# Attention and two MLP layers on one core: the next block's x is loaded at positions 1 and 6, and the weight jobs follow a table

## The chip, the core and the metric

The kernel runs on one core of one Trainium2 chip. The metric is the device time of the whole program in microseconds (us), the median of three runs. TensorE (PE, with its weight loads as PEld) does the matrix products, VectorE (DVE) and ScalarE (ACT) the elementwise work and the copies out of PSUM, SyncE (SP) issues every DMA. Each engine works through its own list of instructions strictly in order: an instruction that waits holds all that stands behind it.

## The reference

`x` is [8, 8, 512, 64] and `state` [8, 8, 32, 64]; the weights are [512, 2048] and [2048, 512], once for each of two MLP layers.

```
xread = softmax(x @ state^T / 8) @ state
sread = softmax(state @ x^T / 8) @ x
x     = concat([xread, sread]) as 4608 tokens x 512
x     = (s * relu(x @ w_in)^2 + b) @ w_out        # first layer
out   = relu(x @ w_in2)^2 @ w_out2                # second layer
```

## The kernel before

**Precision.** Every float32 product is made of reduced-precision pieces: a value is split into a high part (ACT copies it into the narrower type, "hi") and a low part (DVE subtracts that from the value, "lo"), and a product is three matmuls: hi by hi, hi by lo, lo by hi. So each operand that goes into a product costs one ACT and one DVE instruction first, and TensorE waits for both.

**First layer.** It runs in 144 steps; step i handles one token block j (512 tokens) and one slice f of 128 hidden columns (`order`, line 994). From step 32 on, 16 steps make a block. A step is, in this order: six matmuls `mm1` (L509) into a PSUM tile h; on ACT relu, square and the hi copy of it (`relu2`, L516 to L518); twelve matmuls `mm2` (L539) of the slice of step i-2; and then the side work of that step. The PSUM tiles of h, of the attention's transposes and of the S products share four banks in rotation, so a product can start only when the tile four places before it has been read out.

The side work is entered by `at_step(i, fn, rank)` (L998) and runs in the order of rank within its step. It holds the attention of the next block (`att_exp`, `att_norm`, `att_an`, `att_tp`: two DVE transposes and their split stand at places 11 and 12 of a block, the transposes on TensorE at 13), the product S of state and weights (`s_mm`, L306, split at L115 and L116), the lo part of the step's own slice (`low`, L522, rank 5.5), 32 additions that sum up the columns of w_out (`add_up`, L272) and 16 weight jobs.

A weight job (`sums_job`, L196) prepares one piece of the second layer's weights, which arrive as 64-bit floats: load two raw tiles; for each a magnitude on ACT (L131) and four DVE operations that clamp, shift and set bits (L140 to L151, together a `cut`); four DVE sums of 256 columns (`add`, L240); four hi copies on ACT (L249), four lo subtractions on DVE (L253) and eight stores to DRAM. Before the change, job n starts at step 30 + 6n and all of its operations keep the same distances; cuts, add and hi copies stand at ranks 8 to 8.7, behind the step's other work.

**Second layer.** It works on 34 tiles of 128 tokens in six blocks of 6 tiles (the last has 4) with a seven-product scheme in place of eight (`PRODUCTS`). For each block 8 units of seven products each run first (`product`, L751); then follow 24 positions that only add up results (`share`, L775), which I call the share stage: six matmuls of 384 columns each position, twelve in the first three. The stage's position k uses the kept value e = k (t0 to t4 hold them, five a tile); its hi copy (`g_hi`) stands at position k - 3 and its lo at k - 2. At position k the weights for a place 12 further on are loaded into a ring of 12 slots as soon as the slot is read.

During the share stage the x of the next block is prepared (`ahead`, L935): `x_take` (L692) loads it in two parts of two DMAs each into t0 and t1, whose kept values have been read by then; for the second block the bias is added (`x_bias`, L699, on ACT); `x_sum` makes three sums and a difference on DVE, and `xm_hi` and `xm_lo` split the seven operands on ACT and DVE. All of these are entered at fixed positions after k0, the stage's first, behind the pieces of that position. At position 8 ACT also copies a finished result (`p4`), at 16 another.

Of the kernel before, what the change touches and what calls it, by code (L numbers as in the profile page):

```python
# [27 lines left out]
F32 = mybir.dt.float32  # L28
# [12 lines left out]
P = 128  # L41
# [18 lines left out]
TILES = [(j, t) for j in range(B) for t in range(S // P)]  # L60
TILES[2 * TPB : 2 * TPB] = [(B, t) for t in range(NSR // P)]
PARTS = [TILES[i : i + TPB] for i in range(0, len(TILES), TPB)]

LEAST = 2.0 ** (0x70 - 127) * 65536
MOST = (2 - 2.0**-3 - 2.0**-23) * 2.0 ** (0x8F - 127) * 65536
# [3 lines left out]
def attn_mlp2(ctx: ExitStack, tc: tile.TileContext, xT, xn, st, w_in1, w_out1, w_in2, w_out2, s_in, b_in, out):  # L69
# [63 lines left out]
    def to_f32(*pairs):  # L133

        for dst, raw in pairs:
            nc.vector.tensor_scalar(out=dst, in0=dst, scalar1=LEAST, scalar2=MOST, op0=ALU.max, op1=ALU.min)  # L140
        for dst, raw in pairs:
            d = dst.bitcast(U32)
            nc.vector.tensor_scalar(out=d, in0=d, scalar1=3, scalar2=None, op0=ALU.logical_shift_left)
        for dst, raw in pairs:
            d = dst.bitcast(U32)
            nc.vector.scalar_tensor_tensor(  # L146
                out=d, in0=raw[..., 1], scalar=0x80000000, in1=d, op0=ALU.bitwise_and, op1=ALU.bitwise_or
            )
        for dst, raw in pairs:
            d = dst.bitcast(U32)  # L150
            nc.vector.scalar_tensor_tensor(  # L151
                out=d, in0=raw[..., 0], scalar=29, in1=d, op0=ALU.logical_shift_right, op1=ALU.bitwise_or
            )

    def load_piece(key, src, q, k):
        if key[0] == "o":
# [36 lines left out]
        st.update(key=key, mag=mag, pair=lambda: (st["v"], raw), hi=hi, lo=lo)  # L193
        return st

    def sums_job(key, u):  # L196

        c = {}

        def load():  # L200
            c["raw"] = []
            for d in range(2):
                raw = rawp.tile([P, 512, 2], U32, tag="raw", name=f"{key}r{u}{d}")
                if key == "i2":
                    to = raw.rearrange("p (f i c) t -> p f i (c t)", f=2, i=2)
                    for i in range(2):
                        k = 2 * d + i
                        src = w_in2.bitcast(U32)[k * P : (k + 1) * P, 4 * u * P : 4 * (u + 1) * P]
                        nc.sync.dma_start(out=to[:, :, i], in_=src.rearrange("p (f c) -> p f c", f=2))
                else:  # L210
                    f = 2 * u + d
                    nc.sync.dma_start(
                        out=raw.rearrange("p c t -> p (c t)"), in_=w_out2.bitcast(U32)[f * P : (f + 1) * P]
                    )
                c["raw"].append(raw)
            c["v"] = []

        def cut(d):
            v = vp.tile([P, 512], F32, tag="v", name="v")
            c["v"].append(v)  # L220
            magnitude(v, c["raw"][d])
            to_f32((v, c["raw"][d]))

        def four(t):
            return t.rearrange("p (e c) -> p e c", e=2)

        def add():
            v0, v1 = (four(v) for v in c["v"])
            s = vp.tile([P, 512], F32, tag="v", name="v")
            c["v"].append(s)  # L230
            s = four(s)
            c["h"] = [rawp.tile([P, 4, 2 * P], F32R, tag="raw", name=f"{key}h{u}{e}") for e in range(2)]
            s4 = c["h"][1][:, 3].bitcast(F32)
# [7 lines left out]
            h0, h1 = c["h"]  # L241
            c["parts"] = (
                (v0, h0[:, 0:2], slice(0, 5, 4)), (v1, h0[:, 2:4], slice(2, 7, 4)),
                (s, h1[:, 0:2], slice(1, 4, 2)), (h1[:, 3:4].bitcast(F32), h1[:, 2:3], slice(5, 6)),
            )

        def hi(e):
            v, h, _ = c["parts"][e]
            nc.scalar.activation(out=h, in_=v, func=ACTF.Copy)  # L249

        def lo(e):
            v, h, _ = c["parts"][e]
            nc.vector.tensor_tensor(out=v.bitcast(F32R), in0=v, in1=h.bitcast(F32), op=ALU.subtract)  # L253

        def store(e):
            v, h, where = c["parts"][e]
            to = wi_dr[u][:, where] if key == "i2" else wo_dr[:, where, u]
            nc.sync.dma_start(out=to[:, :, 0], in_=h.bitcast(F32))
            nc.sync.dma_start(out=to[:, :, 1], in_=v)

        return load, cut, add, hi, lo, store

    wsum = sraw[:, :, 4 * NS :]

# [519 lines left out]
    def second_layer(rest):  # L784
# [97 lines left out]
        def results(n):  # L882

            th = half(n)
            k0 = first_of[n, NU]
            end = n + 1 == len(PARTS)
            c = {}

            def copies(name, p):
                def fn():  # L890
                    for t in range(2):
                        c[name, t] = c_tile(op, "o", th)
                        act(c[name, t], acc[p, t][:, :th], ACTF.Copy)
# [24 lines left out]
            job(k0 + 16, copies("u2", 1))  # L918
            for t in range(2):
                job(k0 + 20 + t, lambda t=t: add("u2", 3)(c["u2", t], t))  # L920
            nxt = k0 + 24
            for t in range(2):
                go, put = final("u2", t, 1, 0, add("u2", 2))
                job(nxt, go)
                job(nxt + 1, put)
            if end:
                job(nxt + 3, copies("p5", 2))
                return c, final
            job(nxt + 6, copies("u3", 1))
            for t in range(2):  # L930
                go, put = final("p4", t, 0, 1, lambda v, t: sub(v, c["u3", t], v))
                job(nxt + 9, go)
                job(nxt + 10, put)
                go, put = final("u3", t, 1, 1, add("u3", 2))
                job(nxt + 10, go)  # L935
                job(nxt + 11, put)

        def ahead(n):

            k0 = first_of[n - 1, NU]  # L940
            for d in range(2):
                job(k0 + 4 + 4 * d, lambda d=d: x_take(n, d))
                if n == 1:
                    job(k0 + 7 + 4 * d, lambda d=d: x_bias(d))
            for e, k in enumerate((14, 16, 25, 26)):
                job(k0 + k, lambda e=e: x_sum(n, e))
            for m, hi, lo in ((0, 8, 9), (2, 12, 13), (5, 13, 15), (1, 17, 18), (3, 20, 22), (4, 26, 27), (6, 27, 28)):
                job(k0 + hi, lambda m=m: xm_hi(n, m))
                job(k0 + lo, lambda m=m: xm_lo(n, m))

# [101 lines left out]
    jobs1 = [(key, u) for key in ("i2", "o2") for u in range(NU)]  # L1052
    for n, (key, u) in enumerate(jobs1):
        load, cut, add, hi, lo, store = sums_job(key, u)
        t = place[1, CUTS[1]] + 10 + 6 * n
        at_step(t, load, 7)
# [209 lines left out]
```

## Time and profile before

| what | us |
|---|---|
| median of 3 runs (1386.71 to 1393.24) | 1391.29 |
| profiled execution, its own time | 1387.76 |
| its span, first to last instruction | 1385.9 |
| TensorE busy in the span | 1342.6 |
| DVE busy | 943.1 |
| ACT busy | 824.1 |

The profile describes one execution. A line of the waits names who waited for whom, the total, the number of times and the longest. In a timeline, brackets give the engine's idle time before the instruction and what ended it. Line numbers are those of the kernel before. A line of the windows is start:end and length, then the busy time (instructions) of PE, PEld, DVE, ACT and POOL, then PEclk, the DMA engines' busy share and GB/s. "PEclk" is the clock granted to TensorE as a share of full speed.

### The profile page before, as it was taken

Reading aid. Unit: us, or ns where it says so; the run is one execution under the profiler, and the core shown is the slowest. Engines: PE = TensorE matmul, PEld = TensorE weight load, DVE = VectorE, ACT = ScalarE, POOL = GpSimd, SP = SyncE. Lnnn points to the kernel's source line nnn. Section 1 sums busy time; section 2 is a strip of 40 time slices with the busy share of each in tenths; the row PEclk is TensorE's granted clock in tenths of the full one; section 3 lists DMA queues with packets and bytes.
Section 4 is the critical chain, followed back from the end, with each engine's and each line's share of the span. In section 5 each row is a group of like instructions: output and inputs, shape, how many; then the busy total and the mean of one; then the engine's idle time right before and its main releaser. Section 6 shows DMA issues by size and latency. Waiting matters only on the chain.

```text
span 1385.9 us, 23117 instructions
## 1 busy us (share of the span) xinstructions
PE 1342.6 (97%) x8214; PEld 1186.5 (86%) x8214; DVE 943.1 (68%) x1847; ACT 824.1 (59%) x1620; POOL 0.7 (0%) x7
## 2 busy tenths in 40 slices
PE   6899999999999999999999999999999999999998
PEld 4677777777767777788999899989999998999998
DVE  7888667877575767655656586667568666766765
ACT  4777556666666665766655655545555554555555
POOL 0000000000000000000000000000000000000000
PEclk7999999999999999999999999999999999999999
DMA  7365224362526253334586786687668668766987
GB/s 243 115 225 190 92 70 148 107 202 84 203 98 217 92 175 118 116 136 129 191 283 178 222 247 194 168 257 242 178 208 260 200 172 250 242 180 205 302 268 236
DMA packets 159602, 257.91 MB, mean 186 GB/s; under 512 B 14592, under 2 KB 69888, under 8 KB 158720
## 3 DMA queue, kind: packets, MB, share of 16 engines
q1 hardware_dynamic: 159488, 256.44, 58.8%
q8 instruction: 66, 1.08, 0.3%
q14 instruction: 48, 0.39, 0.1%
HBM read 207.09 MB, written 49.28 MB: 185 GB/s over the span
## 4 chain that ended last, share of the span: by engine, by line
PE 82%; DVE 9%; DMA 4%; ACT 3%; issue 1%; SPq 0%; DVEq 0%; POOLq 0%; POOL 0%; ACTq 0%
PE m L751 24%; PE acc L539 22%; PE p L775 21%; PE h L509 12%; DMA bigt<-x 3%; PE S L306 1%; DVE g L522 1%; DMA wi<-v 1%; PE on L1159 1%; DVE S L116 1%; PE sr L461 1%; DVE s L420 1%; DVE v L146 1%; PE sc L306 0%; DVE t L424 0%
## 5 line engine op out<-in xcount | busy, mean ns | idle before, releaser
L539 PE MATMUL acc<-g,o1h 128*128 128x512 f32 (+1 forms) x1152 | 344.8, 381 | 5.6 <-DVE g L522 5.1
L539 PEld LDWEIGHTS acc<-g,o1h 128*128 128x128 f32 x1152 | 212.6, 189 | 50.1 <-DVE g L522 6.6
L539 PE MATMUL acc<-g,o1l 128*128 128x512 f32 (+1 forms) x576 | 218.4, 379 | 0.6 <-DVE o1l L191 0.6
L509 PE MATMUL h<-aT,S 128*128 128x512 f32 x768 | 204.0, 401 | 5.3 <-DVE aT L435 2.9
L751 PE MATMUL m<-bigx,bigx 128*128 128x384 f32 (+1 forms) x1050 | 199.1, 327 | 0.0
L509 PEld LDWEIGHTS h<-aT,S 128*128 128x128 f32 x768 | 142.5, 191 | 60.7 <-issue 9.1
L751 PEld LDWEIGHTS m<-bigx,bigx 128*128 128x128 f32 x1050 | 177.5, 188 | 0.2 <-DVE bigx L593 0.2
L522 DVE TENSOR_TENSOR g<-r,g 128x512 fp32r<-128x512 f32 (+1 forms) x144 | 94.7, 658 | 76.0 <-ACT g L518 75.7
L590 ACT ACTIVATE sc<-sc 128x384 f32<-128x384 f32 (+1 forms) x144 | 72.8, 505 | 102.1 <-DVE sc L593 100.6
L516 ACT ACTIVATE r<-h 128x512 f32<-128x512 f32 (+1 forms) x144 | 81.9, 569 | 82.0 <-PE h L509 78.5
L539 PEld LDWEIGHTS acc<-g,o1l 128*128 128x128 f32 x576 | 108.9, 189 | 21.4 <-DVE o1l L191 1.1
L751 PE MATMUL m<-bigx,bigring 128*128 128x384 f32 (+1 forms) x660 | 124.9, 326 | 0.0
L775 PE MATMUL p<-g,bigw 128*128 128x384 f32 (+1 forms) x522 | 111.9, 326 | 0.0
L751 PEld LDWEIGHTS m<-bigx,bigring 128*128 128x128 f32 x660 | 111.0, 188 | 0.2 <-DVE bigx L593 0.2
L590 ACT ACTIVATE v<-m 128x384 f32<-128x384 f32 (+1 forms) x96 | 45.5, 474 | 91.9 <-PE m L751 91.2
L593 DVE TENSOR_TENSOR v<-m,r 128x384 f32<-128x384 f32 (+1 forms) x48 | 25.7, 535 | 103.8 <-PE m L751 103.8
L517 ACT ACTIVATE r<-r 128x512 f32<-128x512 f32 (+1 forms) x144 | 87.7, 609 | 4.6
L518 ACT ACTIVATE g<-r 128x512 fp32r<-128x512 f32 (+1 forms) x144 | 87.6, 609 | 4.6
L775 PEld LDWEIGHTS p<-g,bigw 128*128 128x128 f32 x522 | 89.7, 189 | 0.0
L116 DVE TENSOR_TENSOR S<-S,S 128x512 fp32r<-128x512 f32 x54 | 34.8, 686 | 69.5 <-ACT S L115 69.5
L775 PE MATMUL p<-g,bigx 128*128 128x384 f32 (+1 forms) x396 | 77.1, 335 | 3.9 <-ACT g L590 2.7
L775 PE MATMUL p<-bigg,bigw 128*128 128x384 f32 (+1 forms) x342 | 73.8, 326 | 0.0
(164 smaller groups left out, 2095.5 us busy)
## 6 DMA issues: line engine op xcount, KB each, us to landing
bigx<-wi SPq DMA_DIRECT2D x200, 256.0 KB, 3.1
bigring<-wi SPq DMA_DIRECT2D x110, 256.0 KB, 3.1
bigx<-wo SPq DMA_DIRECT2D x108, 256.0 KB, 3.1
bigring<-wo SPq DMA_DIRECT2D x66, 256.0 KB, 3.1
i1r<-w_in SPq DMA_DIRECT2D x16, 512.0 KB, 5.2
xn<-xn SPq DMA_DIRECT2D x8, 1024.0 KB, 8.7
o1r<-w_out SPq DMA_DIRECT2D x16, 512.0 KB, 4.3
x<-ot SPq DMA_DIRECT2D x32, 256.0 KB, 3.0
```

The source lines that it names most:

```text
L116: nc.vector.tensor_tensor(out=lo, in0=src, in1=hi.bitcast(F32), op=ALU.subtract)
L146: nc.vector.scalar_tensor_tensor(out=d, in0=raw[..., 1], scalar=0x80000000, in1=d, op0=ALU.bitwise_and, op1=ALU.bitwise_or)
L509: nc.tensor.matmul(out=hp, lhsT=l_, rhs=r_, start=(i == 0), stop=(i == len(ops) - 1))
L516: nc.scalar.activation(out=r, in_=hp, func=ACTF.Relu)
L517: nc.scalar.activation(out=r, in_=r, func=ACTF.Square)
L518: nc.scalar.activation(out=g[:, 0], in_=r, func=ACTF.Copy)
L522: nc.vector.tensor_tensor(out=g[:, 1], in0=r, in1=g[:, 0].bitcast(F32), op=ALU.subtract)
L539: nc.tensor.matmul(out=o, lhsT=l_, rhs=r_, start=(opens and i == 0), stop=(closes and i == 2))
L590: nc.scalar.activation(out=c, in_=src, func=func)
L593: nc.vector.tensor_tensor(out=out, in0=x, in1=y, op=op)
L751: nc.tensor.matmul(out=o, lhsT=w[:, a, k, :], rhs=x[:, b, k, :], start=(start and k + a + b == 0), stop=(k + a == 2), skip_group_check=True,)
L775: nc.tensor.matmul(out=o, lhsT=w[:, a], rhs=g[:, b], start=(opens and e == 0), stop=(u == NU - 1 and e == 2), skip_group_check=True,)
```

## The change

The work on each operand and TensorE's own list stay what they are. Moved are: the two x loads of the share stage from positions 4 and 8 to 1 and 6; the bias from 7 and 11 to 9 and 15; the x sums from 14, 16, 25, 26 to 12, 18, 22, 25; the splits of the seven operands; one addition of results by a position. In the first layer `to_f32` is cut in two (`clamp`, `bits`), and every operation of every weight job has its own step from a table of 16 rows of 15 numbers; the loads stand three steps ahead of the magnitude, the stores one step behind each lo. Hi part 1 may stand before `add`. The third tile of a job, and in every second job also the second, is taken from the pool "o" of four buffers, which also serves the block results, instead of "v" with three. The 32 column additions get steps of a table too.

```
+SUMS_AT = (
+    (27, 27, 27, 27, 28, 28, 34, 35, 30, 35, 35, 36, 35, 36, 36),
+    (31, 31, 31, 34, 34, 35, 39, 40, 38, 41, 41, 42, 40, 42, 43),
...
+        def temp(e):
+            pool, tag = (op, "o") if e == 2 or (e == 1 and n % 2) else (vp, "v")
+            v[e] = pool.tile([P, 512], F32, tag=tag, name="v")
...
+        steps = []
+        for d in range(2):
+            pair = lambda d=d: (v[d], c["raw", d])
+            steps += [lambda d=d: mag(d), lambda p=pair: clamp(p()), lambda p=pair: bits(p())]
+        steps += [add]
+        steps += [lambda e=e: hi(e) for e in range(4)]
+        steps += [lambda e=e: lo(e) for e in range(4)]
+        return load, steps, store
...
-                job(k0 + 4 + 4 * d, lambda d=d: x_take(n, d))
+                job(k0 + (1, 6)[d], lambda d=d: x_take(n, d))
                 if n == 1:
-                    job(k0 + 7 + 4 * d, lambda d=d: x_bias(d))
-            for e, k in enumerate((14, 16, 25, 26)):
+                    job(k0 + (9, 15)[d], lambda d=d: x_bias(d))
+            for e, k in enumerate((12, 18, 22, 25)):
                 job(k0 + k, lambda e=e: x_sum(n, e))
-            for m, hi, lo in ((0, 8, 9), (2, 12, 13), (5, 13, 15), (1, 17, 18), (3, 20, 22), (4, 26, 27), (6, 27, 28)):
+            for m, hi, lo in ((0, 9, 10), (3, 12, 13), (2, 16, 17), (1, 19, 20), (4, 25, 26), (5, 26, 27), (6, 27, 28)):
...
-    for k in range(32):
-        at_step(place[1, CUTS[1]] + 1 + 9 * k // 8, lambda k=k: add_up(k), 6)
+    for k, n in enumerate(ADDS_AT):
+        at_step(n, lambda k=k: add_up(k), 6)
...
+    for n, when in enumerate(SUMS_AT):
+        load, steps, store = sums_job(n)
         for d in range(2):
-            at_step(t + 2 + d, lambda cut=cut, d=d: cut(d), 8)
-        at_step(t + 4, add, 8)
+            at_step(when[3 * d] - 3, lambda load=load, d=d: load(d), 7)
+        for e, (t, fn) in enumerate(zip(when, steps)):
+            at_step(t, fn, 8 + (e == 6) / 2 + (7 <= e < 11) / 4)
         for e in range(4):
-            at_step(t + 4 + e // 2, lambda hi=hi, e=e: hi(e), 8.5)
-            at_step(t + 5 + e // 2, lambda lo=lo, e=e: lo(e), 8.7)
-            at_step(t + 6 + e // 2, lambda store=store, e=e: store(e), 9)
+            at_step(when[11 + e] + 1, lambda store=store, e=e: store(e), 9)
```

**SP in the first share stage.** The DMA list before: `bigring`, `bigg` and `bigx` are ring slots loaded from the weights (`wo`), `bigt0` and `bigt1` take the next block's x.

```order
L648 DMA bigring_6397<-wo_120 128x512 x4
L648 DMA bigg_6653<-wo_120 128x512
L648 DMA bigx0_6105<-wo_120 128x512
L697 DMA bigt0_6554<-x1_1_122 128x2x256
L697 DMA bigt0_6554<-x1_2_123 128x2x512
L648 DMA bigx1_6106<-wo_120 128x512
L648 DMA bigx2_6107<-wo_120 128x512
L902 DMA out_0<-o_7545 128x384
L648 DMA bigx3_6238<-wo_120 128x512
L902 DMA out_0<-o_7547 128x384
L648 DMA bigx4_6239<-wo_120 128x512
L697 DMA bigt1_6555<-x1_1_122 128x2x256
```

The same place of SP's list now:

```order
L682 DMA bigring_6397<-wo_120 128x512 x3
L731 DMA bigt0_6554<-x1_1_122 128x2x256
L731 DMA bigt0_6554<-x1_2_123 128x2x512
L682 DMA bigring_6397<-wo_120 128x512
L682 DMA bigg_6653<-wo_120 128x512
L682 DMA bigx0_6105<-wo_120 128x512
L682 DMA bigx1_6106<-wo_120 128x512
L682 DMA bigx2_6107<-wo_120 128x512
L936 DMA out_0<-o_7545 128x384
L731 DMA bigt1_6555<-x1_1_122 128x2x256
```

The first part of x stands three ring loads earlier, the second part two.

**ACT in the first share stage.** Before: `g0`, `g1`, `g2`, `bigg` are hi copies of kept values, `o` a result, `bigx` an operand of the next block, `bigt0<-bigt0,cs` the bias.

```order
L590 ACTIVATE g2_6772<-bigt2_6618 128x384
L703 ACTIVATE bigt0_6554<-bigt0_6554,cs_109 128x768 x2
L590 ACTIVATE o_7631<-p40_7516 128x384
L590 ACTIVATE o_7633<-p41_7520 128x384
L590 ACTIVATE g0_6659<-bigt2_6618 128x384
L590 ACTIVATE bigx0_6105<-bigt0_6554 128x768
L590 ACTIVATE bigg_6653<-bigt2_6618 128x384 x2
```

Now:

```order
L624 ACTIVATE g2_6772<-bigt2_6618 128x384
L624 ACTIVATE o_7631<-p40_7516 128x384
L624 ACTIVATE o_7633<-p41_7520 128x384
L624 ACTIVATE g0_6659<-bigt2_6618 128x384
L624 ACTIVATE bigg_6653<-bigt2_6618 128x384
L737 ACTIVATE bigt0_6554<-bigt0_6554,cs_109 128x768 x2
L624 ACTIVATE bigx0_6105<-bigt0_6554 128x768
L624 ACTIVATE bigg_6653<-bigt2_6618 128x384
```

The first instruction that needs x has moved behind the result's copies and two more hi copies of kept values.

**DVE at steps 75 and 76 of the first layer.** Before: `v_3845` and `v_3881` are the two raw tiles of weight job 7, `v_3916` its sum, `an` the attention's transposes, `g` the lo part of a slice.

```order
L140 TENSOR_SCALAR v_3881<-v_3881 128x512
L143 TENSOR_SCALAR v_3881<-v_3881 128x512
L146 SCALAR_TENSOR_TENSOR v_3881<-i2r71_3753,v_3881 128x512
L151 SCALAR_TENSOR_TENSOR v_3881<-i2r71_3753,v_3881 128x512
L430 STREAM_TRANSPOSE an_3911<-t1_3741 128x512
L435 TENSOR_TENSOR aT5_3875<-an_3911,aT5_3875 128x512
L522 TENSOR_TENSOR g_3895<-r_3894,g_3895 128x512
L240 TENSOR_TENSOR v_3916<-v_3845,v_3881 128x256
```

Now (the job's tiles are `v_3698`, `v_3735` and the sum `v_3896`):

```order
L165 SCALAR_TENSOR_TENSOR v_3735<-i2r71_3598,v_3735 128x512
L170 SCALAR_TENSOR_TENSOR v_3735<-i2r71_3598,v_3735 128x512
L464 STREAM_TRANSPOSE an_3884<-t1_3688 128x512
L469 TENSOR_TENSOR aT5_3883<-an_3884,aT5_3883 128x512
L556 TENSOR_TENSOR g_3867<-r_3866,g_3867 128x512
L265 TENSOR_TENSOR v_3896<-v_3698,v_3735 128x256
L265 TENSOR_TENSOR v_3896<-v_3896,v_3698 128x256
L265 TENSOR_TENSOR v_3698<-v_3698 128x256
L265 TENSOR_TENSOR i2h71_3894<-v_3735,v_3896 128x256
L464 STREAM_TRANSPOSE an_3925<-t1_3767 128x512
```

The job's add has moved ahead of the second transpose; its second tile is finished before the first one.

## Rows read from the trace of the kernel before

**Rows 1.** The page: busy time, share of the span and instructions of each engine.

```profile
PE 1342.6 (97%) x8214; PEld 1186.5 (86%) x8214; DVE 943.1 (68%) x1847; ACT 824.1 (59%) x1620; POOL 0.7 (0%) x7
```

**Rows 2.** Waits of TensorE: who, for whom, us in total, times, longest.

```profile
PE p L775 <- ACT g L590: 8.5, 4, 3.2
```

**Rows 3.** Windows, first-layer blocks from step 32: length, busy (instructions), clock, DMA.

```profile
191.33:268.53 77.20, 75.11 (x443) 57.82 (x441) 60.06 (x114) 45.10 (x80) 0.00 (x0) 0.98 0.40 131
268.53:344.89 76.36, 74.83 (x451) 57.53 (x449) 54.64 (x103) 50.79 (x91) 0.00 (x0) 1.00 0.43 145
344.89:424.16 79.27, 75.92 (x443) 57.59 (x442) 50.84 (x98) 48.49 (x86) 0.00 (x0) 0.98 0.44 152
424.16:497.95 73.79, 73.49 (x443) 56.66 (x441) 49.93 (x97) 47.74 (x84) 0.00 (x0) 1.00 0.41 138
497.95:573.17 75.22, 73.78 (x443) 56.66 (x441) 49.98 (x94) 49.87 (x89) 0.00 (x0) 1.00 0.43 146
```

**Rows 4.** Windows: ten positions of the first share stage, then five whole stages.

```profile
772.68:786.23 13.55, 13.55 (x79) 13.55 (x79) 9.49 (x20) 7.54 (x17) 0.00 (x0) 1.00 0.61 176
772.68:806.90 34.22, 30.44 (x163) 27.77 (x163) 23.46 (x44) 22.56 (x45) 0.00 (x0) 1.00 0.75 232
895.44:928.93 33.49, 30.90 (x163) 29.45 (x163) 23.37 (x44) 19.48 (x41) 0.00 (x0) 0.95 0.75 236
1017.45:1050.69 33.24, 30.07 (x163) 27.82 (x163) 23.36 (x44) 19.48 (x41) 0.00 (x0) 1.00 0.76 238
1139.21:1173.21 34.00, 31.17 (x163) 29.09 (x163) 23.37 (x44) 19.49 (x41) 0.00 (x0) 0.95 0.77 233
1261.73:1292.54 30.81, 29.32 (x164) 27.82 (x163) 21.79 (x44) 18.41 (x41) 0.00 (x0) 1.00 0.76 239
```

**Rows 5.** Timeline, first share stage: start us, us, engine, instruction [idle before].

```profile
781.64 1.36 SPq L697 DMA_DIRECT2D bigt<-x  x2
...
787.64 1.76 ACT L703 ACTIVATE bigt<-bigt,cs 128x768 f32<-128x768 f32 x2 [5.01 <-DMA bigt<-x]
...
790.04 0.52 ACT L590 ACTIVATE g<-bigt 128x384 fp32r<-128x384 f32 x1
...
790.62 1.57 PE L775 MATMUL p<-g,bigring 128*128 128x384 f32 x6 [3.18 <-ACT g L590]
```

**Rows 6.** Timeline, fourth share stage, ACT and DVE.

```profile
1156.29 0.84 ACT L590 ACTIVATE bigx<-bigt 128x768 fp32r<-128x768 f32 x1 [4.50 <-DMA bigt<-x]
...
1157.16 0.96 DVE L593 TENSOR_TENSOR bigx<-bigt,bigx 128x768 fp32r<-128x768 f32 x1 [4.78 <-ACT bigx L590]
```

**Rows 7.** DMA issues: count, KB each, median us from issue to landing.

```profile
x<-ot SPq DMA_DIRECT2D x32, 256.0 KB, 3.0
...
bigt<-x SPq DMA_DIRECT2D x10, 512.0 KB, 6.2
```

**Rows 8.** Timeline, first layer, steps 75 to 77.

```profile
405.20 0.42 DVE L140 TENSOR_SCALAR v<-v 128x512 f32<-128x512 f32 x1
...
407.46 0.70 DVE L430 STREAM_TRANSPOSE an<-t 128x512 f32<-128x512 f32 x1
...
410.07 1.21 DVE L240 TENSOR_TENSOR v<-v 128x256 f32<-128x256 f32 x3
...
411.32 1.15 ACT L249 ACTIVATE i2h<-v 128x512 fp32r<-128x512 f32 x2 [2.49 <-DVE v L240]
...
413.00 1.34 PE L306 MATMUL S<-V,st 64*32 64x512 f32 x14 [2.40 <-ACT r L516]
```

**Rows 9.** Windows: after two idle stretches of TensorE, and steps 69 and 70.

```profile
787.00:796.00 9.00, 5.56 (x29) 4.48 (x27) 3.24 (x6) 7.43 (x13) 0.00 (x0) 1.00 0.97 347
915.47:918.88 3.41, 3.41 (x13) 3.41 (x12) 0.70 (x2) 1.30 (x3) 0.00 (x0) 0.50 1.01 378
367.72:378.00 10.28, 10.28 (x70) 7.18 (x69) 5.64 (x11) 6.78 (x12) 0.00 (x0) 1.00 0.60 202
```

**Rows 10.** Timeline, first layer, step 69, ACT.

```profile
370.59 0.66 ACT L131 ACTIVATE v<-i2r 128x512 f32<-128x512 f32 x1 [3.46 <-DMA wi<-v]
```

More of the change, by code (lines that the diff above doesn't have):

```diff
@@ L62 @@
 PARTS = [TILES[i : i + TPB] for i in range(0, len(TILES), TPB)]
+SUMS_AT = (
[16 rows of a table added]
+)
+ADDS_AT = (
+    24, 26, 26, 29, 29, 29, 30, 30, 30, 30, 30, 31, 31, 32, 32, 32, 32, 32, 33, 34, 35, 35, 36, 36,
+    37, 37, 37, 38, 44, 45, 46, 46,
+)
 LEAST = 2.0 ** (0x70 - 127) * 65536
@@ L143, in to_f32, with bits @@
             nc.vector.tensor_scalar(out=d, in0=d, scalar1=3, scalar2=None, op0=ALU.logical_shift_left)
+    def bits(*pairs):
         for dst, raw in pairs:
@@ L153, in to_f32 @@
             )
+    def to_f32(*pairs):
+        clamp(*pairs)
+        bits(*pairs)
     def load_piece(key, src, q, k):
@@ L194, in piece, with sums_job, load, mag @@
         return st
-    def sums_job(key, u):
+    def sums_job(n):
+        key, u = ("i2", "o2")[n // NU], n % NU
         c = {}
[L200 to L224, printed above, removed]
+        v = c["v"] = [None] * 3
+        def load(d):
+            raw = c["raw", d] = rawp.tile([P, 512, 2], U32, tag="raw", name=f"{key}r{u}{d}")
+            if key == "i2":
+                to = raw.rearrange("p (f i c) t -> p f i (c t)", f=2, i=2)
+                for i in range(2):
+                    k = 2 * d + i
+                    src = w_in2.bitcast(U32)[k * P : (k + 1) * P, 4 * u * P : 4 * (u + 1) * P]
+                    nc.sync.dma_start(out=to[:, :, i], in_=src.rearrange("p (f c) -> p f c", f=2))
+            else:
+                f = 2 * u + d
+                nc.sync.dma_start(
+                    out=raw.rearrange("p c t -> p (c t)"), in_=w_out2.bitcast(U32)[f * P : (f + 1) * P]
+                )
+        def temp(e):
+            pool, tag = (op, "o") if e == 2 or (e == 1 and n % 2) else (vp, "v")
+            v[e] = pool.tile([P, 512], F32, tag=tag, name="v")
+        def mag(d):
+            temp(d)
+            magnitude(v[d], c["raw", d])
+        def two(t):
@@ L225, in four, with his @@
             return t.rearrange("p (e c) -> p e c", e=2)
+        def his():
+            if "h" not in c:
+                c["h"] = [rawp.tile([P, 4, 2 * P], F32R, tag="raw", name=f"{key}h{u}{e}") for e in range(2)]
+            return c["h"]
         def add():
[L228 to L232, printed above, removed]
@@ L233, in add @@
-            s4 = c["h"][1][:, 3].bitcast(F32)
+            temp(2)
+            v0, v1, s = (two(x) for x in v)
+            s4 = his()[1][:, 3].bitcast(F32)
             for out, x, y, fn in (
@@ L240, in add, with part @@
                 nc.vector.tensor_tensor(out=out, in0=x, in1=y, op=fn)
[L241 to L245, printed above, removed]
+        def part(e):
+            h0, h1 = his()
+            if e == 3:
+                return h1[:, 3:4].bitcast(F32), h1[:, 2:3], slice(5, 6)
+            h = (h0[:, 0:2], h0[:, 2:4], h1[:, 0:2])[e]
+            return two(v[e]), h, (slice(0, 5, 4), slice(2, 7, 4), slice(1, 4, 2))[e]
         def hi(e):
-            v, h, _ = c["parts"][e]
-            nc.scalar.activation(out=h, in_=v, func=ACTF.Copy)
+            x, h, _ = part(e)
+            nc.scalar.activation(out=h, in_=x, func=ACTF.Copy)
         def lo(e):
-            v, h, _ = c["parts"][e]
-            nc.vector.tensor_tensor(out=v.bitcast(F32R), in0=v, in1=h.bitcast(F32), op=ALU.subtract)
+            x, h, _ = part(e)
+            nc.vector.tensor_tensor(out=x.bitcast(F32R), in0=x, in1=h.bitcast(F32), op=ALU.subtract)
         def store(e):
-            v, h, where = c["parts"][e]
+            x, h, where = part(e)
             to = wi_dr[u][:, where] if key == "i2" else wo_dr[:, where, u]
             nc.sync.dma_start(out=to[:, :, 0], in_=h.bitcast(F32))
-            nc.sync.dma_start(out=to[:, :, 1], in_=v)
-        return load, cut, add, hi, lo, store
+            nc.sync.dma_start(out=to[:, :, 1], in_=x)
+        steps = []
[6 more added lines that the diff above has]
+        return load, steps, store
     wsum = sraw[:, :, 4 * NS :]
@@ L919, in results @@
             for t in range(2):
-                job(k0 + 20 + t, lambda t=t: add("u2", 3)(c["u2", t], t))
+                job(k0 + 21 + t, lambda t=t: add("u2", 3)(c["u2", t], t))
             nxt = k0 + 24
@@ L1048, in attn_mlp2 @@
             at_step(step(B, 0) + 4 * q + k - 6, lambda q=q, k=k: lo_v1(q, k), 5)
-    for k in range(32):
-        at_step(place[1, CUTS[1]] + 1 + 9 * k // 8, lambda k=k: add_up(k), 6)
+    for k, n in enumerate(ADDS_AT):
+        at_step(n, lambda k=k: add_up(k), 6)
     at_step(step(BIASED, 0) + 14, lambda: colsum(), 2)
[L1052 to L1056, printed above, removed]
+    for n, when in enumerate(SUMS_AT):
+        load, steps, store = sums_job(n)
         for d in range(2):
-            at_step(t + 2 + d, lambda cut=cut, d=d: cut(d), 8)
-        at_step(t + 4, add, 8)
+            at_step(when[3 * d] - 3, lambda load=load, d=d: load(d), 7)
+        for e, (t, fn) in enumerate(zip(when, steps)):
+            at_step(t, fn, 8 + (e == 6) / 2 + (7 <= e < 11) / 4)
         for e in range(4):
-            at_step(t + 4 + e // 2, lambda hi=hi, e=e: hi(e), 8.5)
-            at_step(t + 5 + e // 2, lambda lo=lo, e=e: lo(e), 8.7)
-            at_step(t + 6 + e // 2, lambda store=store, e=e: store(e), 9)
+            at_step(when[11 + e] + 1, lambda store=store, e=e: store(e), 9)
     def cut_sread():
```

2 lines of the change are left out of this document (1 added, 1 removed), and 14 rows, old and new, of the table SUMS_AT.

## The prediction

> **What bounds the kernel now.** I read the page's first part first: TensorE is busy 1342.6 of 1385.9 us [rows 1], and the change leaves its list alone. So the time can only move by what TensorE loses between its instructions. The waits of TensorE come next: the largest sum in them is 8.5 us in four waits of the share stage on ACT's hi copies [rows 2]. Gaps alone do not tell what is lost, since matmuls that are fed just in time count as busy while they stretch. So I took the length of equal stretches of work from the windows, with the ends read off TensorE's timeline.
>
> First layer: four of the five blocks from step 32 show the same 443 matmuls, the fourth needs 73.79 us and 73.49 of them busy [rows 3]. Against 73.49 the five blocks lose 3.71, 2.87, 5.78, 0.30 and 1.73, together 14.39 us.
>
> Share stages: the first ten positions of the first stage, 78 matmuls, take 13.55 us [rows 4], which is 0.1737 each. A stage to its end has 162 (three positions of 12, 21 of 6), so 28.14 us. The five stages take 34.22, 33.49, 33.24, 34.00 and 30.81 [rows 4] and lose 6.08, 5.35, 5.10, 5.86 and 2.67, together 25.06 us.
>
> So 39.45 us are within this change's reach. The work itself stays, so against the profiled execution's own 1387.76 us the floor is 1348.3. The median shown, 1391.29, is 3.5 higher; I add nothing for that, since a kernel with fewer stalls has fewer of them to vary.
>
> Here the Trainium skill bears on how to count: "Perfetto Trace Analysis", in "Identifying the Most-Contended Engine", says that the busy share of matmuls is no good measure of how near TensorE is to its limit and points to the weight loads. The third stage agrees: PE is busy 30.07 of 33.24 us, PEld 27.82, near the 28.14 of my count [rows 4]. By PE's idle time alone only 8.72 us (first layer) and 13.86 us (stages) would be in reach.
>
> **The x loads, step by step.** The first part of x is issued at 781.64 and the bias behind it starts when it has landed, at 787.64; ACT stood idle 5.01 us for it, since 782.63. Behind it stands the hi copy that TensorE needs, which starts at 790.04, and TensorE starts again at 790.62 after 3.18 us of idling [rows 5]. In the fourth stage, without a bias, it is the x copy that waits 4.50 us, since 1151.79 [rows 6]. I take that as the cause in all five stages.
>
> Now the load stands at position 1 instead of 4. Position 4 ends 48 matmuls after k0, at 781.0, and the issue came 0.6 later. Position 1 ends after 24 matmuls, at 4.17; with the same 0.6 the load is issued 4.8 us after k0, in the first stage at 777.4. With the 6.0 from issue to use it is there at 10.8 after k0. As an upper bound I take both issues (1.36 [rows 5]) and the median landing of 6.2 [rows 7] one after the other, 7.6: then it is there at 12.4. Its first user has moved behind the result's copies and two hi copies. In the fourth stage ACT was ready for the x copy at 1151.79 - 1139.21 = 12.58 after the stage's start, with one hi copy (0.52 [rows 5]) less ahead of it, so now at 13.1. The load is 0.7 to 2.3 us early; ACT waits for nothing there.
>
> The second part is issued at the end of position 6 (60 matmuls, 10.42, plus 0.6 is 11.0) and is there by 18.6 at most. Its first user stands at position 15 (18.8) or 16 (19.8). Both fit, the first barely. The ring loads that the x loads now pass on SP are 12 positions ahead of their use, and the first positions last twice as long; I cost this at nothing. If that cover went, a late slot would show as TensorE waiting for a DMA.
>
> What is late next? After the x copy (0.84) and its own 0.52 the next hi copy is done at 14.5, and with DVE's 0.96 for the x lo [rows 6] ahead of it the piece's lo about 15.5. Position 13 needs it at 96 matmuls, 16.7. So stages two to five hold, with 1 us to spare; I leave 0.3 each, 1.2. The first stage also has two biases of 1.76 [rows 5]: hi at 16.2, lo at 17.2, and the third matmul needs it at 17.0. From there ACT and DVE are at the limit, with three more splits and the second bias to come. The bounds are 0 and all of 6.08 left; I take 2.5. So 25.06 - 3.7 = 21.4 us come back.
>
> **The weight jobs.** The longest gap of the third block shows what is wrong. DVE cuts the job's second tile from 405.20, turns the attention's second half from 407.46 and only then, at 410.07, makes the job's add. ACT's hi copies wait for the add until 411.32, and behind them stands the read-out of h, whose PSUM bank TensorE needs: it starts at 413.00 after 2.40 us, that is, it could have started at 410.60 [rows 8]. In the new list the cut (2.26) is already done and the turn with the slice's lo (2.61) stands behind the add. So the add starts 4.87 us earlier, at 405.2, and is done at about 406.7. The turn follows, with ACT's half of it done by 408.1; the two hi copies (1.15) and a short one (0.4) end at 409.7 and the read-out at 410.3, before 410.60. This gap goes, with little to spare.
>
> The other gaps have the same form: DVE gets a cut and an add in the very steps where the attention fills it. On average there is room, since DVE is busy 50 to 60 us of a block [rows 3]. A load that comes late does no harm by itself: ACT waited 3.46 us for one in step 69 [rows 10], and TensorE was busy throughout steps 69 and 70 [rows 9].
>
> New in the table is a wait: the result copies of a block need four "o" buffers, and a job still holds one or two. In four blocks (steps 49, 65, 81, 97) the fourth copy, on ACT, takes the buffer of the first and waits for its store, 3.0 us in the median [rows 7]. Behind it stand the split of S and the next relu. At steps 49 to 52 the load of job 4 stands behind the attention's loads as well. Bounds: 0, since the 3.46 above cost nothing, and 4 x 3.0 = 12. I take the nearer row and leave 1.6. So 14.39 - 1.6 = 12.8 come back.
>
> **Sum.** 1387.76 - 21.4 - 12.8 = 1353.6; I say 1353.5.
>
> The clock is in these numbers already: after its waits in the second stage TensorE ran from 915.47 at 0.50 of full speed, 1.2 in place of 2.4 GHz, for 3.41 us [rows 9], about 1.7 us lost; after the 3.18 us in the first stage it kept 1.00 [rows 5, 9]. The Trainium skill ("TensorE: Matmul & The Clock Gate", Part 1) has the clock fall when the engine has idled; the trace shows that this need not follow. By the rule alone, 2.5 us left in one gap of the first stage would bring 1.7 more, 1355.2.
>
> **Rivals.**
> The table only moves the stalls. For it: in four blocks a new wait of 3.0, and the margin of 0.3 us at the gap worked out. Against it: in that gap 4.87 us of DVE work leave the way. If all 14.39 stay: 1387.76 - 21.4 = 1366.4.
>
> The share stage stays bound by its pieces. DVE is busy 23.4 us of a stage that is to take 28.14 [rows 4], in a chain with ACT. If half of the 25.06 stays: 1387.76 - 12.5 - 12.8 = 1362.5. Against it: the positions before the x load ran at full speed with DVE 9.49 of 13.55 busy [rows 4].
>
> Only idle time comes back, the stretched matmuls stay: 22.58 less the 5.3 kept above gives 1370.5. Against it: the weight loads' busy time.
>
> It turns slower. From its first magnitude to its last store a job now takes eight to ten steps in place of five and holds its buffers; if the next job's magnitude, on ACT, waits for a buffer whose store has not landed, relu is held in every job. By the worst gap seen (2.40, and 1.7 of clock) that is 4.1 us in each of 16 jobs, 65.6, in place of 14.39: 1387.76 - 21.4 + 51.2 = 1417.6. It decides from (21.4 + 14.39) / 16 = 2.2 us a job on. Against it: the covered 3.46.
>
> The x loads don't move in time, because DVE reads a kept value of t0 late: then the stages' loss stays, 1387.76 - 12.8 = 1375.0. If the first layer's stays as well, nothing moves, 1384 to 1391.
>
> **Chances.** Forecast 0.65, its own range 1348 to 1360; stalls only moved 0.12; half of the stages' loss stays 0.11; idle time alone 0.03; x loads late 0.02; no change 0.03; slower 0.04. What a measurement can tell from no change is 0.5%, 7 us. Faster 0.65 + 0.12 + 0.11 + 0.03 + 0.02 = 0.93, the same 0.03, slower 0.04. The range 1346 to 1367 takes in the first three cases, and 2 us below the floor for what varies elsewhere.
>
> **What would show it.** The five share stages should take 28 to 29 us, the first about 30.6, and ACT should no longer wait for the DMA of x in any. The blocks of the first layer should take 73.5 to 75, without TensorE idle before S at step 77. Wrong I am if TensorE shows new waits for ACT at the first steps of a block (the "o" buffer), at step 53 (job 4's load), or for pieces from position 13 on in stages without a bias.

## The result, and the profile after

The changed kernel takes 1352.11 us, the median of four runs (1351.20 to 1353.45), against 1389.28 for the kernel before, whose fourth run moved its median from the 1391.29 of three; the ratio is 0.9731, with a 95% interval of 0.9702 to 0.9759. A second group of runs gave 1352.55 against 1389.28. The profiled execution took 1351.20 us with a span of 1349.4, so its span is 36.5 us shorter.

The page's first part answers to [rows 1]. TensorE's busy time has fallen too, by 17.0 us, with the same number of matmuls.

```profile
PE 1325.6 (98%) x8214; PEld 1181.7 (88%) x8214; DVE 942.3 (70%) x1847; ACT 827.8 (61%) x1620; POOL 0.7 (0%) x7
```

The five blocks of the first layer, the changed kernel's windows with the columns of [rows 3]:

```profile
190.37:264.81 74.44, 73.49 (x443) 56.65 (x442) 60.76 (x114) 46.58 (x83) 0.00 (x0) 1.00 0.38 126
264.81:338.96 74.15, 74.15 (x451) 57.60 (x449) 52.83 (x103) 49.18 (x87) 0.00 (x0) 1.00 0.48 162
338.96:413.48 74.52, 73.64 (x443) 56.74 (x441) 50.14 (x97) 48.51 (x86) 0.00 (x0) 1.00 0.44 147
413.48:486.68 73.20, 73.20 (x443) 56.71 (x441) 49.71 (x96) 50.35 (x88) 0.00 (x0) 1.00 0.44 148
486.68:559.88 73.20, 73.20 (x443) 56.72 (x441) 49.68 (x97) 49.51 (x87) 0.00 (x0) 1.00 0.46 155
```

They take 369.51 us together, 12.33 less than before. And the five share stages, which answer to [rows 4]:

```profile
759.43:789.42 29.99, 29.44 (x164) 27.88 (x163) 22.64 (x42) 22.06 (x44) 0.00 (x0) 1.00 0.82 268
877.82:905.90 28.08, 28.08 (x163) 28.08 (x163) 23.11 (x43) 18.99 (x40) 0.00 (x0) 1.00 0.84 282
994.30:1022.51 28.21, 28.21 (x164) 28.06 (x164) 22.66 (x42) 18.99 (x40) 0.00 (x0) 1.00 0.85 282
1110.92:1139.16 28.24, 28.24 (x163) 28.05 (x163) 22.65 (x42) 18.99 (x40) 0.00 (x0) 1.00 0.85 282
1227.57:1255.66 28.09, 28.09 (x164) 28.09 (x164) 21.93 (x44) 18.37 (x40) 0.00 (x0) 1.00 0.80 264
```

They take 142.61 us, 23.15 less. In the waits of TensorE the largest sum of [rows 2] is gone; what is left of a share stage there is one line:

```profile
PE p L809 <- DVE g L627: 0.5, 2, 0.3
```

Read the first two numbers of a stage's row against each other: in the last four stages PE is busy for the whole length and the length is that of the work, 28.1; no clock below 1.00 is left in either table. 12.33 + 23.15 = 35.48 of the 36.5 us. The other 1.0 lies outside both and is the net of small shifts, among them the start (the first layer's first matmul stands 0.7 us earlier) and the last share stage, which has grown by 0.4.

Why the stages are short is seen in the fourth one, where ACT had waited 4.50 us [rows 6]. The timeline of the changed kernel, SP's queue and ACT:

```profile
1115.69 0.90 SPq L731 DMA_DIRECT2D bigt<-x  x2
...
1123.36 0.52 ACT L624 ACTIVATE g<-bigt 128x384 fp32r<-128x384 f32 x1
1123.78 0.84 ACT L624 ACTIVATE bigx<-bigt 128x768 fp32r<-128x768 f32 x1
```

The load is issued 4.77 us after the stage's start and its first user starts at 12.86, straight behind the copy before it: no idle time in brackets, so nothing was waited for.

At steps 75 to 77 the order of [rows 8] is turned round. The changed kernel's timeline:

```profile
398.67 1.21 DVE L265 TENSOR_TENSOR v<-v 128x256 f32<-128x256 f32 x3
...
400.14 0.70 DVE L464 STREAM_TRANSPOSE an<-t 128x512 f32<-128x512 f32 x1
...
402.45 0.40 ACT L276 ACTIVATE i2h<-i2h 128x256 fp32r<-128x256 f32 x1
402.76 0.57 ACT L550 ACTIVATE r<-h 128x512 f32<-128x512 f32 x1
...
403.95 1.09 PE L340 MATMUL S<-V,st 64*32 64x512 f32 x16
```

The add runs ahead of the transpose, the job's last hi copy ends at 402.85, the read-out of h at 403.33, and S starts at 403.95 without a bracket. Of the 2.40 us nothing is left.

### The profile page after: what moved, and what is told of

It is laid out like the page before. It is cut to its first block, busy times and chain, and to the rows that moved or that the text cites. A ratio compares the mean times of both kernels' runs of the same rounds, so it can differ in the third digit from the quotient of the medians.

```text
span 1349.4 us, 23118 instructions
## 1 busy us (share of the span) xinstructions
PE 1325.6 (98%) x8214; PEld 1181.7 (88%) x8214; DVE 942.3 (70%) x1847; ACT 827.8 (61%) x1620; POOL 0.7 (0%) x7
## 4 chain that ended last, share of the span: by engine, by line
PE 91%; DVE 6%; ACT 2%; issue 1%; DMA 0%; DVEq 0%; POOLq 0%; POOL 0%; ACTq 0%
PE p L809 25%; PE m L785 25%; PE acc L573 25%; PE h L543 13%; PE S L340 2%; PE on L1189 1%; PE sr L495 1%; PE sc L340 0%; PE tp L475 0%; PE S L368 0%; DVE t L443 0%; DVE m L442 0%; DVE S L138 0%; DVE t L438 0%; DVE g L556 0%
## 5 line engine op out<-in xcount | busy, mean ns | idle before, releaser
L556 DVE TENSOR_TENSOR g<-r,g 128x512 fp32r<-128x512 f32 (+1 forms) x144 | 94.6, 657 | 74.1 <-ACT g L552 74.1
L809 PE MATMUL p<-g,bigx 128*128 128x384 f32 (+1 forms) x396 | 73.7, 328 | 0.6 <-DVE g L627 0.5
```

The source lines that it names most:

```text
L556: nc.vector.tensor_tensor(out=g[:, 1], in0=r, in1=g[:, 0].bitcast(F32), op=ALU.subtract)
L809: nc.tensor.matmul(out=o, lhsT=w[:, a], rhs=g[:, b], start=(opens and e == 0), stop=(u == NU - 1 and e == 2), skip_group_check=True,)
```

## The experiments

Medians in us, each beside the kernel before on the same chip (1388.69, 1389.30 and 1389.28 in the three groups); "blocks" and "stages" are the sums of the five windows in the profiled execution. The changed kernel's time is that of the last group, its sums are those shown above.

| kernel | time | ratio, 95% interval | blocks | stages |
|---|---|---|---|---|
| before | 1389.28 | | 381.84 | 165.76 |
| changed | 1352.55 | 0.9732 [0.9715, 0.9748] | 369.51 | 142.61 |
| share stage alone | 1363.60 | 0.9821 [0.9804, 0.9839] | 381.60 | 142.32 |
| table alone | 1378.00 | 0.9918 [0.9902, 0.9935] | 369.26 | 167.32 |
| loads alone | 1372.98 | 0.9882 [0.9861, 0.9903] | 382.41 | 150.48 |
| loads put back | 1362.39 | 0.9807 [0.9791, 0.9823] | 369.69 | 153.91 |
| old adds | 1355.07 | 0.9755 [0.9738, 0.9771] | 371.84 | 142.39 |
| new adds, old jobs | 1365.57 | 0.9821 [0.9805, 0.9838] | 381.74 | 142.60 |

**The two halves apart.** First the share stage on the kernel before:

```diff
-                job(k0 + 4 + 4 * d, lambda d=d: x_take(n, d))
+                job(k0 + (1, 6)[d], lambda d=d: x_take(n, d))
...
-            for e, k in enumerate((14, 16, 25, 26)):
+            for e, k in enumerate((12, 18, 22, 25)):
```

> The kernel before with the share-stage half of the change alone (loads of x at positions 1 and 6, its users moved, the result's second copy one position later); the weight jobs stay as they were. Theory: the two halves work in different stages and add up. The five share stages should be as long as in the changed kernel, 28.1 to 28.3 us and the first 30.0, so 23.1 us less than before, and the first layer's blocks as before, 73.5 to 79.3: 1389.3 - 23.1 = 1366. Rival, the stalls of the first layer also cost the second through the clock or late buffers: the stages keep some of their 25 us and the time is above 1370. Rival, the table carries most of the gain: 1376 or more.

Then the changed kernel with these lines put back:

> The changed kernel with the share stage put back (loads at 4 and 8 and every user where it was); the weight jobs follow the table. Theory: the five blocks of the first layer come out as in the changed kernel (74.4, 74.2, 74.5, 73.2, 73.2), 12.3 us less than before, the share stages as before (34.2, 33.5, 33.2, 34.0, 30.8): 1389.3 - 12.3 = 1377. The sum of the two halves' gains should then be 35.4 of the 37.2 measured. Rival, the stall only moves without the other half: within 3 us of before.

Each half gives back its own stretch: 25.1 and 10.7 us, together 35.8 of 37.2. With the share stage alone the blocks are as before. With the table alone the stages keep all that they lost and take 1.6 us more; 1.1 of that is in the first, where the granted clock is 0.90 in the mean and not 1.00 as before [rows 4]:

```profile
759.35:794.65 35.30, 30.82 (x163) 30.41 (x163) 23.52 (x44) 22.75 (x45) 0.00 (x0) 0.90 0.73 225
```

The first theory holds in both: the halves add up, and no stall of the first layer shows in the second. (What moved by one position in the first of them is DVE's add of the result, not a copy.)

**The load, or the order of its users?** On the kernel before only the first pair of lines above; and on the changed kernel the same pair put back.

> The kernel before with nothing changed but the two loads of x, at positions 1 and 6; the bias, splits and sums stay at their old places. Theory (the load's landing holds ACT): the wait for the first part goes in all five stages. The second part is issued 11.0 us after the stage's start and lands at 17.2 to 18.6, while its first hi copy stands at position 12, whose end is at 16.7: ACT may wait there up to 1.9 us, and the pieces behind it lose about 1 us a stage. So 5 to 10 of the 25.06 us stay, 15 to 20 come back: 1369 to 1374. Rival (the order of the work on ACT and DVE is the cause, the load only shows it): the stages stay at 31 to 34 us, 1385 to 1390. Rival (the load alone is all of it): 28 to 30 us a stage, 1366.

> The changed kernel with the two loads of x back at positions 4 and 8; their users stay where the change put them, as does the table. Theory (the landing decides): the first part is issued 9.0 us after the stage's start and lands at 15.0, ACT is ready for it at 13.1 and waits 1.9 us; position 13 needs its piece at 16.7 and it had about 1 us to spare, so each stage loses about 1 us, the first 3 to 4 in all: 1352.1 + 6 = 1358. Rival (the order alone is enough, since the users moved behind the landing): the stages as in the changed kernel, within 2 us of 1352. Rival (the load's place is everything): the stages back at 31 to 34, 1373 or more.

The stages lose 9.8 us against 5 x 28.14 with the loads alone, and 13.2 with the users alone; before they lost 25.06. So neither is the whole: the loads alone bring 15.3 us, the users alone 11.9, and both 23.15, less than their sum, since they remove parts of one wait. With the loads alone it is the second part that is late: ACT waits 2.9 to 3.7 us for it in each of the five stages, where up to 1.9 was expected, and 0.7 for the first part in the first stage only. Its second stage, SP's queue and ACT:

```profile
904.66 0.96 SPq L697 DMA_DIRECT2D bigt<-x  x2
...
911.96 0.85 ACT L590 ACTIVATE bigx<-bigt 128x768 fp32r<-128x768 f32 x1 [3.66 <-DMA bigt<-x]
```

The landing as the cause is borne out; in the second kernel the size was wrong, 13.2 where 6 was expected. Its fourth stage shows where, in the timeline:

```profile
1127.31 0.90 SPq L731 DMA_DIRECT2D bigt<-x  x2
...
1135.43 0.84 ACT L624 ACTIVATE bigx<-bigt 128x768 fp32r<-128x768 f32 x1 [4.09 <-DMA bigt<-x]
...
1136.73 0.62 PE L809 MATMUL p<-g,bigring 128*128 128x384 f32 x2 [1.55 <-ACT g L624]
```

The issue came 8.94 us after the stage's start, as worked out (9.0), and ACT was ready at 1135.43 - 4.09 = 1131.34, or 12.97 (13.1). But 8.1 us passed from issue to use, not the 6.0 of the first stage of before. The wait for a load is not one number, and the trace of before had shown it already. Its fourth stage, whose use at 1156.29 stands in [rows 6], has this issue:

```profile
1148.17 1.39 SPq L697 DMA_DIRECT2D bigt<-x  x2
```

That is 8.1 us too; in the five stages of before ACT used the first part 6.0, 7.7, 7.2, 8.1 and 6.8 us after its issue.

**What is left in the first stage.** The changed kernel keeps 1.85 us there. Its timeline, all engines:

```profile
779.78 1.75 ACT L737 ACTIVATE bigt<-bigt,cs 128x768 f32<-128x768 f32 x2
...
782.17 0.52 ACT L624 ACTIVATE g<-bigt 128x384 fp32r<-128x384 f32 x1
...
782.72 0.56 DVE L627 TENSOR_TENSOR g<-bigt,g 128x384 fp32r<-128x384 f32 x1 [1.69 <-ACT g L624]
...
784.94 2.30 PE L809 MATMUL p<-g,bigx 128*128 128x384 f32 x10 [0.28 <-DVE g L627]
```

The second pair of biases holds ACT, the next piece's hi copy ends at 782.69, DVE has idled 1.69 us for it, and from there on the pieces come one by one just as TensorE asks for them. Three kernels ask whether it is the bias: without it, on GpSimd, and split between ACT and DVE.

```diff
-            nc.scalar.activation(out=v, in_=v, func=ACTF.Identity, bias=cs[:, k : k + 1])
+            nc.gpsimd.tensor_scalar(out=v, in0=v, scalar1=cs[:, k : k + 1], scalar2=None, op0=ALU.add)
```

> The changed kernel, with the bias of the first share stage's x left out (four ACT instructions of 0.88 us; the second part's tokens then lack the bias). Theory (ACT's two biases of 1.75 us are what makes the pieces late there): the first stage falls from 29.99 to 28.1 to 28.3 us like the other four, everything else as it was: 1.8 us less, about 1350. Rival (the first stage is late for another reason, for instance a later landing of its loads): it stays above 29 us.

> The changed kernel with the first share stage's four bias instructions on GpSimd, which does nothing else there. No row of the traces shows GpSimd on a tile of this size. Theory (ACT's load is the limit): with 3.5 us less on ACT the stage takes 28.1 to 28.6. Rival (the bias lies in the chain from the landing to the piece, so it is its own length that counts, and GpSimd shares time with DVE): 30 to 33 us; with 2 us or more for one instruction the x copy at position 9 is held by over 2 us and the stage is longer than now.

> The changed kernel with one of the two bias instructions of each load on DVE and the other on ACT, side by side. DVE gains about 0.63 us for each (0.42 us for 128x512 in the first layer, by columns), ACT loses 0.88. Theory (ACT's load and the chain's length): the first stage takes 28.3 to 29.2 instead of 29.99, so about 1 us less than the changed kernel. Rival (DVE, with 23.4 us of work in 28.1, is as close to its limit): it stays within 0.3 of 29.99 or grows.

With the bias on ACT the stage took 29.96 to 29.99 us in six traces. Without the bias it takes 28.09, so the bias is all of it. On GpSimd it takes 31.70. GpSimd's and ACT's timeline there:

```profile
770.89 4.39 POOL L737 TENSOR_SCALAR bigt<-bigt,cs 128x768 f32<-128x768 f32 x2 [769.56 <-DMA bigt<-x]
...
775.31 0.85 ACT L624 ACTIVATE bigx<-bigt 128x768 fp32r<-128x768 f32 x1 [2.83 <-POOL bigt L737]
```

2.2 us for one, and the x copy behind them waits for 2.83: the rival was right, the bias lies in the chain. Split in two it is short on both engines, and the window shows 28.32 us for the stage:

```profile
759.23:787.55 28.32, 28.32 (x164) 28.09 (x163) 23.69 (x44) 20.41 (x42) 0.00 (x0) 1.00 0.84 283
```

The kernel without the bias ran in 1351.46 us, the one on GpSimd in 1352.22, the split one in 1350.70. None is told from the changed kernel by its time; here the windows decide.

**What is left in the blocks.** At step 43 TensorE idles 0.95 us in the changed kernel:

```profile
240.93 0.14 DVE L451 TENSOR_SCALAR s<-s 128x1 f32<-128x1 f32 x1
...
242.39 0.69 DVE L458 TENSOR_TENSOR t<-t,s 128x512 f32<-128x512 f32 x1
...
243.00 0.68 DVE L556 TENSOR_TENSOR g<-r,g 128x512 fp32r<-128x512 f32 x1
243.60 0.15 DVE L451 TENSOR_SCALAR s<-s 128x1 f32<-128x1 f32 x1
243.73 0.19 PEld L573 LDWEIGHTS acc<-g,o1h 128*128 128x128 f32 x1 [1.37 <-DVE g L556]
243.73 0.50 PE L573 MATMUL acc<-g,o1h 128*128 128x512 f32 x1 [0.95 <-DVE s L451]
```

For the matmul the trace names the norm (L451) as the releaser. But it reads g's lo part, which DVE finished at 243.68, behind the norm's six instructions; its weight load, which starts with it, is put down to that lo part (L556). So one rank was changed:

```diff
-    rank = {..., att_exp: 5, att_norm: 5}
+    rank = {..., att_exp: 5, att_norm: 5.6}
```

> The changed kernel with one rank changed: in each step DVE takes the lo part of the slice ahead of the attention's norm and not behind it. Theory (at steps 43 and 75 TensorE waits because the lo part stands behind six norm instructions, 2.1 us): the losses of 1.24 and 0.54 us there go, the blocks from steps 32 and 64 take 73.2 and about 74.0 and the kernel is 1.8 us shorter, about 1350. Rival (DVE is simply full there): the norm, which is now later, makes the next transposes late, and the loss of 1 to 2 us moves to steps 44 to 45 and 76 to 77.

The first and third block in its windows:

```profile
190.31:263.69 73.38, 73.25 (x442) 56.72 (x441) 60.73 (x113) 46.03 (x82) 0.00 (x0) 1.00 0.39 128
...
337.85:412.28 74.43, 73.38 (x442) 56.79 (x441) 50.15 (x97) 48.49 (x86) 0.00 (x0) 1.00 0.44 148
```

The first block gains 1.06 us, as the theory has it; the third only 0.09, since there 0.5 us come back at step 77, as the rival has it. The time is 1351.91, not told from the changed kernel.

**Jobs or adds?** The table moves the jobs' operations and the column sum's 32 adds. One kernel has the old adds under the new table, the other the new adds (and the share stage's half) beside the old jobs.

```diff
-    for k, n in enumerate(ADDS_AT):
-        at_step(n, lambda k=k: add_up(k), 6)
+    for k in range(32):
+        at_step(place[1, CUTS[1]] + 1 + 9 * k // 8, lambda k=k: add_up(k), 6)
```

> The changed kernel with the 32 adds of the weights' column sum back at their old steps (one a step from 21 to 55, so one of 0.7 us in each of steps 41, 42 and 43, where DVE is late already); the jobs keep their table. Theory (in the first block it is these adds, between the attention's norm and the slices, that cost 2.7 of its 4.0 us at step 43): the block from step 32 goes back to 76 to 77.2 us, the block from step 48 by less than 0.5, the others stay: 1352.1 + 2.5 = 1354.6. Rival (the jobs' operations alone decide): the blocks as in the changed kernel, within 0.5 us each.

> The kernel before with the share-stage half of the change and the new places of the 32 adds, without the jobs' table. Theory: the block from step 32 comes down from 77.2 to about 74.5, the others stay at 76.2, 79.2, 73.8 and 75.2: 1363.6 - 2.7 = 1361. Rival (the jobs' operations alone decide): all five blocks as in the kernel before, 1363.6. Rival (adds and jobs hold each other up): the first block keeps over 2 of its 4.0 us here.

My theory fell in both. The time with the old adds, 1355.07 where 1354.6 was expected, came out by luck: it is another block that is longer. With the old adds the first block stays at 74.36 and the second goes to 76.71; with the new adds beside the old jobs the first block takes 77.40, no less than before. So the jobs' table carries the gain, and the adds' new places keep 2.3 us of it (371.84 - 369.51), in the second block, where before the table the adds did not show. Which part of the table does it, the new steps of DVE's operations, the earlier loads or the tiles from "o", was not taken apart; that it is DVE's order rests on the timeline of steps 75 to 77. The changed kernel's repeat in this group:

> The changed kernel unaltered, run beside the others of this group. Every theory expects 1351 to 1353, with the first share stage at 30.0 us and the five blocks at 74.4, 74.2, 74.5, 73.2 and 73.2.

It gave 1352.55 us, with stages of 29.99 and 28.1 and blocks as before it.

**A version that beats both.** The split bias, the norm behind the lo part, and one more line. In the last share stage ACT copies a result, p5, into "o" tiles whose stores are still under way; in the kernel with the changed rank that held ACT for 4.61 us and TensorE for 2.40:

```profile
1343.36 0.70 ACT L624 ACTIVATE o<-p 128x256 f32<-128x256 f32 x2 [4.61 <-DMA out<-o]
```

```diff
-                job(nxt + 3, copies("p5", 2))
+                job(nxt + 3, copies("p5", 2, vp, "v"))
```

> The changed kernel with three things: DVE takes the slice's lo part ahead of the attention's norm (worth 1.1 us in the blocks), one bias of each load on DVE (1.7 us in the first share stage), and in the last share stage the copies p5 take tiles that nobody holds, and not the buffers whose stores are still under way. ACT waited 0.2 to 4.6 us there for a store to land, and the stage took 25.5 to 28.9 us in the runs so far, 25.9 in the changed kernel's trace. Theory: 25.5 each time, 1.14 + 1.67 + 0.4 = 3.2 us less than the changed kernel, about 1349, and a smaller spread between runs. Rival (the copies wait for something else): the last stage still varies.

It takes 1347.81 us (1347.36 to 1348.60), ratio 0.9699 [0.9685, 0.9714], 4.7 us less than the changed kernel beside it (1350.69 to 1354.43), where 3.2 were expected; that kernel's last stage had taken 27.09 us in this group and not 25.92. Its copies go to v, and its last share stage is as long as its work:

```profile
1336.66 0.64 ACT L624 ACTIVATE v<-p 128x256 f32<-128x256 f32 x2
```

```profile
1315.93:1341.45 25.52, 25.52 (x212) 25.20 (x210) 16.75 (x46) 15.91 (x45) 0.00 (x0) 1.00 0.77 250
```

That stage took 25.53 us in the trace of before, 25.92 and 27.09 in the two of the changed kernel and 29.98 in the one with the old adds, where ACT waited 5.13 us for a store. A store that lands late thus explains part of the spread between runs: the four runs of this version lie within 1.2 us, the five of the changed kernel beside it within 3.7.

## Why the prediction was right, step by step

The time was forecast at 1353.5, by a sum of 1353.6 for the profiled execution; that took 1351.20, and the median is 1352.11. The mechanism was the forecast's: both halves give back nearly all that their stretches lost. The terms:

- **The share stages, 21.4 forecast, 23.15 measured.** Loss by the length of equal stretches (25.06) and not by idle time (13.86) was the right measure: 23.15 came back, more than all the idle time. The Trainium skill's advice to read the weight loads ("Perfetto Trace Analysis", "Identifying the Most-Contended Engine") is borne out: PEld was busy 27.82 us in the third stage before and 28.06 after, while PE's busy time fell from 30.07 to 28.21.
- **The x load.** Issue forecast at 4.8 us after the start, measured 4.77; ACT ready at 13.1, measured 12.86 without a wait. That the ring loads behind the x loads cost nothing held: in the changed kernel's trace TensorE waits for no DMA in a share stage. The margin was smaller than worked out. The 6.0 from issue to use was the shortest of five, and the fourth stage's 8.1 lies above the upper bound of 7.6; with it the load is there 12.9 us after the start, 0.2 ahead of 13.1 and not 0.7.
- **What is kept there, 3.7 forecast, 1.91 measured.** 2.5 for the stage with the bias against 1.85, and 1.2 for the other four against 0.06. The cause named, ACT's bias, is shown by the kernel without it; the pieces late are those from position 13 on.
- **The blocks, 12.8 forecast, 12.33 measured.** They keep 2.06 us over 5 x 73.49 where 1.6 was forecast, but this term is right by accident. Its base was off as well: 73.49 is not the work of a block, since the fourth and fifth now take 73.20, and the second holds 0.95 us of column sum that was counted as lost. By that measure the blocks had lost 14.9 us (14.39 in the prediction) and keep 2.6. The gap at step 77 went as worked out: the read-out of h ends 0.6 us before S starts, where 0.3 was forecast. The waits for an "o" buffer came, at all four places, and cost TensorE nothing. The changed kernel's waits of ACT:

```profile
ACT ot L597 <- DMA x<-ot: 4.2, 3, 1.5
...
ACT ot L599 <- DMA x<-ot: 2.5, 1, 2.5
```

  Four waits, 1.3 to 2.5 us long, in steps 49, 65, 81 and 97, and each of these steps, from one product h to the next, takes the 6.22 us that it took in the kernel before. The lower bound, 0, was the right one. What the blocks keep comes from elsewhere: the norm ahead of the lo part (0.95 and 0.24 us idle at steps 43 and 75), eight matmuls of the column sum, which are work (x451 in the second block's row), and one new wait: in step 68 ACT's hi copies waited 2.89 us for a tile whose store, of the job before, had not landed, and in step 69 TensorE idled 0.49 for what stood behind them. Step 69 is long in every trace with the table (6.3 to 6.8 us against 6.05) and in none without it, but its cause is read off the trace and wasn't tried.
- **The rivals.** "The table only moves the stalls" is answered by the blocks: at steps 43, 61 and 77 they shrank or went, and the fourth and fifth block lose nothing. "Half of the stages' loss stays" and "idle time alone" are answered by the stages, "the loads don't move" by the issue at 4.77. The slower rival has its like at this one place, at 0.49 us in one job and not 4.1 in each of 16.
- **The clock.** The stretches at 0.50 that the kernel before had in blocks and stages (one is in [rows 9]) are gone with the gaps; they are within the lengths above and not to be added. No gap over 0.28 us is left in the first stage, so the 1.7 us more that a fall of the clock would have cost there did not arise.

## What to carry to other kernels

Measure what a stage loses by the length of equal work, since matmuls fed just in time hide the loss in busy time; then ask for each wait what stands behind it in its engine's queue. A load moved forward and its users moved back each remove part of the same wait, so their gains don't add. When the large stalls are gone, look for buffers that are reused while a store is in flight, and for an operation that is first in a step only by its rank.

## What the runs showed of the hardware

**The same gap, two clocks.** Behind the gap at step 43 the clock fell in the kernel before, where TensorE had idled 2.10 us, and not in the kernel with the loads alone, where it had idled 2.09; their first layers are the same. The windows of the stretch behind the gap, first before, then loads alone (columns as in [rows 3]):

```profile
245.84:249.25 3.41, 3.40 (x9) 2.75 (x10) 3.27 (x9) 1.86 (x3) 0.00 (x0) 0.59 0.42 147
```

```profile
245.16:248.58 3.42, 3.42 (x15) 2.85 (x16) 3.28 (x9) 1.87 (x3) 0.00 (x0) 1.00 0.42 148
```

The granted clock was mostly 0.50 in the one, 1.2 GHz, and 1.00 in the other, 2.4 GHz; the block took 77.20 us against 76.17. The 3.18 us of [rows 5] cost no clock, and 2.10 did. So in these runs a gap's length alone doesn't tell whether the clock falls; what does was not tried. The Trainium skill ("TensorE: Matmul & The Clock Gate", Part 1) has the clock fall when the engine has idled; the rows agree that it can, and show that it need not.

**GpSimd on a plain add.** 128x768 in f32 took 2.2 us on GpSimd (4.39 for the first two), 0.93 on ACT and 0.61 on DVE. The second two took 6.02, with DVE at work beside them; during the second of the first pair DVE stood idle. The Trainium skill ("GPSIMD Engine Reference", "Engine selection") has one-input operations there at roughly line rate; this trace doesn't agree. Spans on GpSimd are rough, but ACT's wait of 2.83 us for it is not.
